# Attention and two expert layers on one core: inputs turned at a pair's end, the leaky sum kept in PSUM, a respread start and end of the second layer

## The chip, the cores and the metric

The kernel runs on one core of a Trainium2 chip. The metric is the device time of one execution in microseconds. Five engines work side by side, each through its own queue of instructions: TensorE (PE, matmuls and transposes), VectorE (DVE), ScalarE (ACT), GpSimd (POOL) and SyncE (SP, here the one that issues DMAs). Semaphores hold an instruction until what it reads is written and what it overwrites is read.

## The reference, cut to what matters

```python
scores = q @ k.T / 8 - slope * dist       # 2 batches, 8 heads, 768 tokens, 64 columns
a = softmax(where(keep, scores, -1e9))    # 8 global keys and 96 local ones
x = (a @ v)                               # as 1536 tokens x 512

h = x @ w_in                              # first layer: 512 -> 2048
x = (max(h, 0) + alpha * min(h, 0)) @ w_out           # leaky, 2048 -> 512

h = x @ w_in2                             # second layer
P = a0 + a1*h + a2*h**2 + a3*h**3
Q = 1 + abs(b0)*abs(h) + abs(b1)*h**2
out = (P / (Q + 1e-6)) @ w_out2
```

q, k, v and the output are 32-bit floats. The four weight matrices come as 64-bit floats, which the kernel reads and converts itself.

## The kernel before

**Products.** Every factor is split into a high and a low half of reduced width (names end in `hi` and `lo`): the high half is a copy to the narrow type, the low half the difference. A product is then three passes: hi x hi, lo x hi, hi x lo. So each value that enters a product costs one copy (mostly on ScalarE) and one subtraction (mostly on VectorE).

**Attention.** A slot `u` handles two steps `z` of two heads each: `scores` (L432), the mask and the row maxima on VectorE (`biased`, L447), `exponentials` on ScalarE (L454), the row sums on GpSimd (L471) and their reciprocal on VectorE (L472, a 128x4 instruction, one per slot), the scaling by GpSimd (L466). A slot later P is transposed on TensorE (L483, L485), copied from PSUM to `pt` (`copy_p`, L492 and L494), and multiplied with v (`values`, L507 and L509); `store_x` writes the result as `xhi` (ScalarE, L519) and `xlo` (VectorE, L520). New key and query blocks are transposed (`transpose_in`, L400), and `split_in` makes their high half on ScalarE (`khi` L407, `qhi` L410) and their low half on VectorE (L408, L411).

**Opening.** The first ten slots of the attention (`alone`, u = 0 to 9) run without products of the expert layers. From u = 10 on, `joint_slot(s)` (s = 0 to 15, u = 10 + s) weaves one slot of the attention (`opening`, `turning`) with one step of the first layer. Attention ends inside s = 15; then `plain_slot(s)` runs.

**Expert layers.** There are 96 steps: 48 of the leaky layer, 48 of the rational one; a step is a group of 512 tokens and 128 hidden columns. `first(n)` makes the hidden block in one PSUM bank with twelve matmuls (L735); for n below LATE = 16 this is always bank 3, later n % 3. `leaky(n)` forms the activation with two VectorE instructions (L741, L742) in the SBUF tile `act`, ScalarE copies it to `ghi` (L743), and GpSimd subtracts to `glo` (L744). `rational_a` to `rational_e` do the same for the second layer over more instructions (L753 to L786). `second(n)` multiplies with the output weights (L801), twelve matmuls into four banks. At the end of a group `drain` adds the halves of a sum (L826) and makes the next layer's inputs: `xhi` (L834) at once, `xlo` (L835) through the queue `later`.

**Weights.** `tick` is called twice per slot and moves a pipeline of weight loads: ScalarE scales the exponent word (L324, tile `de`), three VectorE instructions join the two words (L313, L314, L315, tile `dx`, called a conversion below), a tick later the high half is copied (L301 on ScalarE, L303 on GpSimd in `alone`), and another tick later VectorE makes the low half (L304). Each tick also runs one entry of `later`. Which ticks start a load stands in the table of `plan_weights`: for the second layer's first weights it names ticks 48 to 95 in part, and then every fifth from 101 on.

**Order.** Nothing is scheduled: the instructions stand on each engine in the order in which the code calls them.

Of the kernel before, what the change touches and what calls it, by code (L numbers as in the profile page):

```python
# [37 lines left out]
JOIN = 20  # L38
# [22 lines left out]
class Kernel:  # L61
# [35 lines left out]
    def arm(self, attention, sfx):  # L97
        tc = self.tc
        self.sfx = sfx
        self.slots = list(self.early)  # L100
        self.pipe, self.join, self.unspilled, self.later, self.splits = (deque() for _ in range(5))
        self.loads = self.started = self.used = 0
        moe = self.moe()
        with tc.tile_pool(name="spill_" + sfx, bufs=1, space=DRAM) as spill:
            self.spilled = [self.alloc_slot(spill, i, "d") for i in range(KEPT)]
            self.saved = {mg: spill.tile([P, NC, DM], F32, name=f"saved{mg[0]}{mg[1]}_{sfx}") for mg in SAVED}
            with tc.tile_pool(name="at_" + sfx, bufs=1) as pool:
                attention(pool, moe)
            with tc.tile_pool(name="late_" + sfx, bufs=1, reuse_waits="tile") as late:
                self.slots += [self.alloc_slot(late, i) for i in range(NEARLY, NF)]  # L110
                moe(None)
# [109 lines left out]
    def plan_weights(self):  # L221
# [26 lines left out]
        times += range(101, 160, 5)  # L248
# [35 lines left out]
    def tick(self, on_act, start, spread=False):  # L284
        nc = self.nc
        if self.later:
            self.later.popleft()()
# [74 lines left out]
    def attention_window(self, pool, moe):  # L362
# [124 lines left out]
        def copy_p(u, first_bank):  # L487
            for z in steps_of(u):
                copy = nc.vector.tensor_copy if z < JOIN - 3 and z % 4 == 0 else nc.scalar.copy
                t = transposed(z, first_bank + z % 2)  # L490
                if width(z) == P:
                    copy(pt[z % 4][:, :, 0], t[:, :, 0])  # L492
                else:
                    copy(pt[z % 4], t)  # L494
# [66 lines left out]

        def alone(u):
# [3 lines left out]
            biased(u)  # L566
            if u < 2:
# [6 lines left out]
            lows = [store_x(u - 3)]  # L574
            for n, (nm, i, cs) in enumerate(inputs(u)):
# [3 lines left out]
                if u < 2:  # L579
                    lows.pop()()  # L580
            keys_of_all(u)
            self.tick(False, t in self.starts, spread=True)
            exponentials(2 * u + 1)
            transpose_p(u - 2, 6)
            for low in lows:
                low()
            self.join_step(3)
            copy_p(u - 2, 6)
# [8 lines left out]
        def opening(u):  # L597
# [3 lines left out]
            biased(u)  # L601
            due = {JOIN // 2: (u - 3,), JOIN // 2 + 1: (u - 3, u - 2)}.get(u, (u - 2,))
# [6 lines left out]
            lows = [store_x(v) for v in due]  # L609
            for z in some[1:]:  # L610
                exponentials(z)
            for low in lows:
                low()

        def turning(u):
# [3 lines left out]
            lows = []  # L619
# [5 lines left out]
            for nm, i, cs in inputs(u):  # L625
                lows.append(split_in(nm, i, 2, cs))
            return lows
# [93 lines left out]
    def moe(self):  # L721
# [16 lines left out]
        def leaky(n):  # L738
# [3 lines left out]
            nc.vector.scalar_tensor_tensor(t, h, 0.0, t, ALU.max, ALU.add)  # L742
            nc.scalar.copy(hi, t)  # L743
            nc.gpsimd.tensor_tensor(lo, t, hi.bitcast(F32), ALU.subtract)  # L744
# [65 lines left out]
        def drain(n, d):  # L810
# [9 lines left out]
            if n == N - 1 and d == 3:  # L820
                for half in (slice(0, DM // 2), slice(DM // 2, DM)):
                    nc.vector.tensor_add(o[:, half], y[:, half], o[:, half])
                    nc.sync.dma_start(out=out[:, half], in_=o[:, half])
# [21 lines left out]
        def joint_slot(s, halves):  # L845
# [6 lines left out]
            opening(u)  # L852
            first(s)
            self.tick(True, 2 * s in self.starts)
            lows = turning(u)
            leaky(s)
            for low in lows:
                low()
            if s:
                second(s - 1)  # L860
            self.tick(True, 2 * s + 1 in self.starts)

        def plain_slot(s):
# [4 lines left out]
            if s < N:  # L868
                first(s)
            if s >= N:  # L870
                final_slot(s)
                return
# [13 lines left out]
            if ready and not steps[early][0]:  # L886
                leaky(early)
            self.tick(True, 2 * s in self.starts)
            if ready and steps[early][0]:
# [85 lines left out]
```

## Time and profile before

| | us |
|---|---|
| median of three runs (661.48, 663.15, 663.91) | 663.15 |
| the profiled execution's own time | 662.42 |
| its span in the profile | 660.62 |
| PE busy | 622.9 (94%) |
| DVE busy | 541.1 (82%) |
| ACT busy | 374.8 (57%) |
| POOL busy | 191.6 (29%) |
| mean granted TensorE clock | 0.987 of full |

Busy shares are means over stages that differ. The page cuts the span into 40 slices of 16.5 us; there TensorE is busy less than nine tenths in slices 1 to 4, 7 and 25 and in the last, and VectorE nine tenths or more in slices 6 to 8 (83 to 132 us), 14, 17, 22 to 26, 28 to 31 and 38. So the reading goes by stages: prelude to 20 us, slots of the attention alone to 59 us, joint slots to about 202 us, leaky slots to about 380 us, the rational layer, the end.

### The profile page before, as it was taken

What the parts mean: (1) busy time and instruction counts of PE and PEld (TensorE: products, weight loads), DVE (VectorE), ACT (ScalarE), POOL (GpSimd) and SP (SyncE); (2) the same over time, 40 slices, a digit from 0 to 9 for tenths busy, and PEclk for the clock granted to TensorE, in tenths of its full rate; (3) what the DMA queues carried; (4) which work ended last, traced back from release to release, by engine and by line L of the source; (5) the groups of instructions that cost most, each with busy time, mean ns of one, the idle gap of its engine ahead of it and who ended that gap; (6) DMA issues with size and microseconds to landing.
All of it is one profiled execution on the core that took longest, in us unless ns stands there. A gap on an engine that the chain in (4) does not pass through costs nothing. (4 is left out here: it accounts for less than half of the span.)

```text
span 660.6 us, 9551 instructions
## 1 busy us (share of the span) xinstructions
PE 622.9 (94%) x3250; PEld 506.3 (77%) x3250; DVE 541.1 (82%) x972; ACT 374.8 (57%) x782; POOL 191.6 (29%) x268
## 2 busy tenths in 40 slices
PE   6777998999999999999999998999999999999994
PEld 6566766778878888888888877878878888888783
DVE  4687899987656987977889999999989877786984
ACT  2785565667643432333333376777777666766662
POOL 4454434333341321222222212222222222222221
PEclk7998999999999999999999999999999999999998
DMA  8879498978777952330522511131110000300302
GB/s 162 192 189 274 145 256 261 269 207 268 255 263 253 353 183 90 103 96 32 165 90 65 158 34 33 36 125 32 33 64 1 1 1 1 127 1 0 129 0 70
DMA packets 84859, 82.82 MB, mean 125 GB/s; under 512 B 45312, under 2 KB 61952, under 8 KB 84800
## 3 DMA queue, kind: packets, MB, share of 16 engines
q1 hardware_dynamic: 84800, 82.11, 41.6%
q8 instruction: 27, 0.44, 0.3%
q14 instruction: 32, 0.26, 0.1%
HBM read 60.21 MB, written 19.92 MB: 121 GB/s over the span
## 5 line engine op out<-in xcount | busy, mean ns | idle before, releaser
L744 POOL TENSOR_TENSOR glo<-act,ghi 128x512 fp32r<-128x512 f32 x48 | 65.6, 1366 | 213.5 <-ACT ghi L743 193.8
L786 POOL TENSOR_TENSOR glo<-act,ghi 128x512 fp32r<-128x512 f32 (+1 forms) x49 | 65.3, 1332 | 201.9 <-ACT ghi L782 180.3
L743 ACT CAST ghi<-act 128x512 fp32r<-128x512 f32 x48 | 29.8, 621 | 104.6 <-DVE act L742 96.7
L735 PE MATMUL bank<-xhi,winhi_f 128*128 128x512 f32 x256 | 68.4, 389 | 0.0
L735 PE MATMUL bank<-xhi,winlo_f 128*128 128x512 f32 x256 | 68.4, 389 | 0.0
L735 PE MATMUL bank<-xlo,winhi_f 128*128 128x512 f32 x256 | 68.4, 389 | 0.0
L454 ACT ACTIVATE prob<-prob,stat 128x232 f32<-128x232 f32 (+1 forms) x96 | 44.7, 468 | 40.2 <-DVE stat L447 40.0
L735 PEld LDWEIGHTS bank<-xhi,winhi_f 128*128 128x128 f32 x256 | 48.1, 188 | 10.0
L735 PEld LDWEIGHTS bank<-xlo,winhi_f 128*128 128x128 f32 x256 | 48.1, 188 | 10.0
L735 PEld LDWEIGHTS bank<-xhi,winlo_f 128*128 128x128 f32 x256 | 48.1, 188 | 10.0
L314 DVE SCALAR_TENSOR_TENSOR dx<-de,dx 128x512 int32<-128x512 int32 x64 | 52.7, 824 | 2.2
L315 DVE SCALAR_TENSOR_TENSOR dx<-stage,dx 128x512 int32<-128x512 int32 x64 | 52.1, 815 | 2.2
L762 DVE SCALAR_TENSOR_TENSOR stage<-stage,abs_b 128x512 f32<-128x512 f32 (+1 forms) x49 | 36.2, 739 | 16.3 <-ACT stage L754 16.3
L753 ACT ACTIVATE stage<-bank 128x512 f32<-128x512 f32 (+1 forms) x49 | 28.8, 587 | 35.7 <-PE bank L735 35.7
L466 POOL TENSOR_SCALAR prob<-prob,rec 128x232 f32<-128x232 f32 (+1 forms) x96 | 42.2, 458 | 16.9 <-DVE rec L472 10.2
L782 ACT CAST ghi<-act 128x512 fp32r<-128x512 f32 (+1 forms) x49 | 30.2, 616 | 27.7 <-DVE act L779 27.7
L324 ACT ACTIVATE de<-stage 128x512 f32<-128x512 f32 x64 | 42.6, 671 | 2.6 <-DMA stage<-in_moe_w_out_dram 2.6
L801 PE MATMUL bank<-wouthi_f,glo 128*128 128x512 f32 x144 | 41.3, 392 | 0.8 <-POOL glo L786 0.7
L801 PE MATMUL bank<-wouthi_f,ghi 128*128 128x512 f32 x144 | 41.3, 392 | 0.6 <-ACT ghi L782 0.6
L313 DVE TENSOR_SCALAR dx<-de 128x512 int32<-128x512 int32 x64 | 38.6, 603 | 3.5 <-ACT de L324 3.5
L801 PE MATMUL bank<-woutlo_f,ghi 128*128 128x512 f32 x144 | 41.0, 389 | 0.0
L777 DVE SCALAR_TENSOR_TENSOR stage<-stage,cq,bank 128x512 f32<-128x512 f32 (+1 forms) x49 | 36.0, 734 | 4.1 <-ACT bank L767 4.1
(208 smaller groups left out, 1466.7 us busy)
## 6 DMA issues: line engine op xcount, KB each, us to landing
stage<-in_moe_w_in_dram SPq DMA_DIRECT2D x32, 512.0 KB, 3.9
stage<-in_moe_w_out_dram SPq DMA_DIRECT2D x32, 512.0 KB, 4.1
part<-saved_f SPq DMA_DIRECT2D x16, 256.0 KB, 4.0
va<-in_v_dram SPq DMA_DIRECT2D x13, 256.0 KB, 5.1
saved_f<-part SPq DMA_DIRECT2D x12, 256.0 KB, 3.5
out_dram<-part SPq DMA_DIRECT2D x11, 256.0 KB, 2.0
rawk<-in_k_dram SPq DMA_DIRECT2D x10, 256.0 KB, 4.6
rawq<-in_q_dram SPq DMA_DIRECT2D x10, 256.0 KB, 4.7
```

The source lines that it names most:

```text
L313: lambda: nc.vector.tensor_scalar(y, e, 3, None, ALU.logical_shift_left),
L314: lambda: nc.vector.scalar_tensor_tensor(y, e, -(2**31), y, ALU.bitwise_and, ALU.bitwise_or),
L315: lambda: nc.vector.scalar_tensor_tensor(y, low, 29, y, ALU.logical_shift_right, ALU.bitwise_or),
L324: nc.scalar.mul(self.de[n % 2], self.staged(n)[:, :, :, 1].bitcast(F32), 2.0**-112)
L454: nc.scalar.activation(p[:, j - e, :w], p[:, j - e, :w], AF.Exp, bias=st[:, j : j + 1], scale=-1.0, accum_out=st[:, 4 + j : 5 + j],)
L466: nc.gpsimd.tensor_scalar(p[:, j, :w], p[:, j, :w], r[:, e + j : e + j + 1], 1.0, ALU.mult, ALU.mult)
L735: nc.tensor.matmul(bk, w["in", a][:, c, :], x[:, c, :], start=e == 0, stop=e == len(seq) - 1)
L744: nc.gpsimd.tensor_tensor(lo, t, hi.bitcast(F32), ALU.subtract)
L762: nc.vector.scalar_tensor_tensor(w, w, self.ab[:, 0:1], ab, ALU.add, ALU.mult)
L777: nc.vector.scalar_tensor_tensor(w, w, self.cq[:, 0:1], r, ALU.add, ALU.mult)
L786: nc.gpsimd.tensor_tensor(lo, u, hi.bitcast(F32), ALU.subtract)
L801: nc.tensor.matmul(y[d], lhs, rhs, start=begin and e == 0, stop=last and e == 2)
```

## The change

Five things are changed.

1. In `alone`, the transposes of new inputs, their high halves and the copies of P stand behind both pairs of exponentials; the low halves of the inputs wait in `lows` until the next slot's row maxima (`opening` of the first joint slot calls them too). A weight's low half then comes directly behind `store_x`'s low half. All copies of P are on ScalarE.
2. In `joint_slot`, both ticks stand between the attention's opening and its turning, one ahead of `first`, one behind.
3. `leaky` writes the sum back to the PSUM bank instead of `act`; ScalarE copies from there, and the subtraction for `glo` is on VectorE, from PSUM, called after the other low halves.
4. `tick` runs an entry of `later` only in every second call; the second layer's late weight starts move from 101, 106, ... to 107, 112, ...
5. At the end, the last step's first product is issued together with the one before it, a slot earlier, and the last half of the output is sent from ScalarE's DMA queue instead of SyncE's.

```diff
-        times += range(101, 160, 5)
+        times += range(107, 160, 5)
...
     def tick(self, on_act, start, spread=False):
-        if self.later:
+        self.ticks += 1
+        if self.later and self.ticks % 2:
             self.later.popleft()()
...
         def copy_p(u, first_bank):
-                copy = nc.vector.tensor_copy if z < JOIN - 3 and z % 4 == 0 else nc.scalar.copy
+                copy = nc.scalar.copy
...
         def alone(u):
             scores(u)
             both_ready(u - 1)
             biased(u)
+            low_halves()
...
             exponentials(2 * u)
-            lows = [store_x(u - 3)]
+            low = store_x(u - 3)
+            self.tick(False, t in self.starts, spread=True)
+            exponentials(2 * u + 1)
+            low()
+            self.join_step(3)
+            transpose_p(u - 2, 6)
+            copy_p(u - 2, 6)
             for n, (nm, i, cs) in enumerate(inputs(u)):
                 bank = (3, 2)[n % 2]
                 transpose_in(nm, i, bank, cs)
                 lows.append(split_in(nm, i, bank, cs))
                 if u < 2:
-                    lows.pop()()
+                    low_halves()
             keys_of_all(u)
-            self.tick(False, t in self.starts, spread=True)
-            exponentials(2 * u + 1)
-            transpose_p(u - 2, 6)
-            for low in lows:
-                low()
-            self.join_step(3)
-            copy_p(u - 2, 6)
             self.tick(False, t + 1 in self.starts, spread=u < JOIN // 2 - 1)
...
         def leaky(n):
             nc.vector.tensor_scalar(t, h, 0.0, self.al[:, fc : fc + 1], ALU.min, ALU.mult)
-            nc.vector.scalar_tensor_tensor(t, h, 0.0, t, ALU.max, ALU.add)
-            nc.scalar.copy(hi, t)
-            nc.gpsimd.tensor_tensor(lo, t, hi.bitcast(F32), ALU.subtract)
+            nc.vector.scalar_tensor_tensor(h, h, 0.0, t, ALU.max, ALU.add)
+            nc.scalar.copy(hi, h)
+            return lambda: nc.vector.tensor_sub(lo, h, hi.bitcast(F32))
...
-                    nc.sync.dma_start(out=out[:, half], in_=o[:, half])
+                    (nc.scalar if half.start else nc.sync).dma_start(out=out[:, half], in_=o[:, half])
...
         def joint_slot(s, halves):
             opening(u)
+            if s:
+                self.tick(True, 2 * s - 1 in self.starts)
             first(s)
             self.tick(True, 2 * s in self.starts)
             lows = turning(u)
-            leaky(s)
-            for low in lows:
-                low()
+            low = leaky(s)
+            for more in lows:
+                more()
+            low()
             if s:
                 second(s - 1)
-            self.tick(True, 2 * s + 1 in self.starts)
+            if s == LATE - 1:
+                self.tick(True, 2 * s + 1 in self.starts)

         def plain_slot(s):
-            if s < N:
+            if s < N - 1:
                 first(s)
+            if s == N - 2:
+                first(s + 1)
...
-            if ready and not steps[early][0]:
-                leaky(early)
+            low = leaky(early) if ready and not steps[early][0] else None
             self.tick(True, 2 * s in self.starts)
+            if low:
+                low()
```

In the rows below, `bank_82` to `bank_89` are the PSUM banks 0 to 7, and line numbers of after are one higher than those of before up to L521, and eight to nine higher in the expert layers.

**ScalarE, one late slot of `alone` with a query block.** Before, from the slot's first exponentials on:

```order
L454 ACTIVATE prob_254,stat_260<-prob_254,stat_260 128x232 x2
L519 CAST xhi_105<-bank_84 128x2x128
L410 ACTIVATE qhi_250<-bank_85 128x512
L324 ACTIVATE de_95<-stage_91 128x512
L454 ACTIVATE prob_255,stat_260<-prob_255,stat_260 128x232 x2
L494 COPY pt_266<-bank_89 128x512
```

After, from the same instruction on:

```order
L455 ACTIVATE prob_254,stat_260<-prob_254,stat_260 128x232 x2
L520 CAST xhi_105<-bank_84 128x2x128
L325 ACTIVATE de_95<-stage_91 128x512
L455 ACTIVATE prob_255,stat_260<-prob_255,stat_260 128x232 x2
L495 COPY pt_265<-bank_88 128x512
L495 COPY pt_266<-bank_89 128x512
L411 ACTIVATE qhi_250<-bank_85 128x512
```

The query's copy moves from between the two pairs of exponentials to behind the copies of P, of which both are here now.

**VectorE, a joint slot with two conversions,** the last twelve instructions up to the reciprocal of the next slot. Before:

```order
L304 TENSOR_TENSOR winlo__112<-dx_97,winhi__111 128x512
L313 TENSOR_SCALAR dx_96<-de_95 128x512
L314 SCALAR_TENSOR_TENSOR dx_96<-de_95,dx_96 128x512
L315 SCALAR_TENSOR_TENSOR dx_96<-stage_91,dx_96 128x512
L741 TENSOR_SCALAR act_100<-bank_85,al 128x512
L742 SCALAR_TENSOR_TENSOR act_100<-bank_85,act_100 128x512
L408 TENSOR_TENSOR klo<-bank_84,khi 128x4x128
L304 TENSOR_TENSOR woutlo__126<-dx_98,wouthi__125 128x512
L313 TENSOR_SCALAR dx_97<-de_94 128x512
L314 SCALAR_TENSOR_TENSOR dx_97<-de_94,dx_97 128x512
L315 SCALAR_TENSOR_TENSOR dx_97<-stage_92,dx_97 128x512
L472 RECIPROCAL rec_264<-rec_264 128x4
```

After:

```order
L314 TENSOR_SCALAR dx_98<-de_94 128x512
L315 SCALAR_TENSOR_TENSOR dx_98<-de_94,dx_98 128x512
L316 SCALAR_TENSOR_TENSOR dx_98<-stage_90,dx_98 128x512
L305 TENSOR_TENSOR winlo__112<-dx_97,winhi__111 128x512
L314 TENSOR_SCALAR dx_96<-de_95 128x512
L315 SCALAR_TENSOR_TENSOR dx_96<-de_95,dx_96 128x512
L316 SCALAR_TENSOR_TENSOR dx_96<-stage_91,dx_96 128x512
L749 TENSOR_SCALAR act_100<-bank_85,al 128x512
L750 SCALAR_TENSOR_TENSOR bank_85<-bank_85,act_100 128x512
L409 TENSOR_TENSOR klo<-bank_84,khi 128x4x128
L752 TENSOR_TENSOR glo_104<-bank_85,ghi_102 128x512
L473 RECIPROCAL rec_264<-rec_264 128x4
```

The second conversion moves from behind the leaky activation to ahead of it, the sum goes to bank 3 instead of `act`, and the subtraction L752 takes the place in front of the reciprocal.

**VectorE, start of the second layer,** from the last addition of halves (L826, after: L834) on; `stage` and `act` are tiles of the rational activation. Before:

```order
L826 TENSOR_TENSOR part_78<-bank_89,part_78 128x512
L835 TENSOR_TENSOR xlo_109<-part_75,xhi_106 128x512
L777 SCALAR_TENSOR_TENSOR stage_92<-stage_92,cq,bank_85 128x512
L778 SCALAR_TENSOR_TENSOR stage_92<-stage_92,bank_85 128x512
L779 SCALAR_TENSOR_TENSOR act_99<-act_99,na,stage_92 128x512
L762 SCALAR_TENSOR_TENSOR stage_93<-stage_93,abs_b 128x512
L835 TENSOR_TENSOR xlo_109<-part_76,xhi_106 128x512
```

After:

```order
L834 TENSOR_TENSOR part_78<-bank_89,part_78 128x512
L785 SCALAR_TENSOR_TENSOR stage_92<-stage_92,cq,bank_85 128x512
L786 SCALAR_TENSOR_TENSOR stage_92<-stage_92,bank_85 128x512
L787 SCALAR_TENSOR_TENSOR act_99<-act_99,na,stage_92 128x512
L770 SCALAR_TENSOR_TENSOR stage_93<-stage_93,abs_b 128x512
L843 TENSOR_TENSOR xlo_109<-part_75,xhi_106 128x512
```

The low half of the first block of activations (`xlo` from `part_75`) moves behind the first piece of the rational activation.

## Rows read from the trace of the kernel before

**Rows 1.** Windows: stretch, length, engines' busy us (operations), TensorE's clock, DMA share, GB/s.
```profile
38.00:60.00 22.00, 15.03 (x159) 12.69 (x160) 20.90 (x62) 15.89 (x51) 11.73 (x26) 0.92 0.85 228
55.90:59.20 3.30, 3.30 (x20) 2.81 (x16) 3.17 (x12) 2.72 (x10) 2.19 (x4) 0.50 0.96 347
78.00:148.00 70.00, 64.67 (x432) 49.03 (x430) 62.62 (x144) 42.20 (x117) 26.80 (x52) 1.00 0.84 246
148.00:200.00 52.00, 51.93 (x369) 41.72 (x366) 31.74 (x88) 30.87 (x83) 21.12 (x37) 1.00 0.80 264
```

**Rows 2.** Timeline, TensorE: start, duration, engine, line, operation, count, [idle before<-releaser].
```profile
147.41 0.38 PE L432 MATMUL bank<-khi,qhi 64*128 64x232 f32 x2
...
149.31 1.20 PE L735 MATMUL bank<-xhi,winhi__115 128*128 128x512 f32 x4
...
156.31 0.38 PE L432 MATMUL bank<-khi,qhi 64*128 64x232 f32 x2
```

**Rows 3.** Timeline, second layer's start: TensorE's two waits, then VectorE.
```profile
391.99 0.73 PE L801 MATMUL bank<-wouthi__113,ghi 128*128 128x512 f32 x2 [1.50 <-ACT ghi L782]
...
405.11 0.72 PE L801 MATMUL bank<-wouthi__121,ghi 128*128 128x512 f32 x2 [1.87 <-ACT ghi L782]
...
388.44 0.68 DVE L835 TENSOR_TENSOR xlo<-part,xhi 128x512 fp32r<-128x512 f32 x1
...
397.88 1.52 DVE L313 TENSOR_SCALAR dx<-de 128x512 int32<-128x512 int32 x1
```

**Rows 4.** Timeline, the end: TensorE, then SyncE's queue.
```profile
634.47 0.84 PE L735 MATMUL bank<-xhi,winhi_f 128*128 128x512 f32 x3
...
652.17 0.39 PE L801 MATMUL bank<-wouthi_f,glo 128*128 128x512 f32 x1
...
653.07 1.44 SPq L823 DMA_DIRECT2D out_dram<-part  x2
```

**Rows 5.** Timeline, opening slot: VectorE's mark, ScalarE's copy and its next.
```profile
37.77 0.18 DVE L472 RECIPROCAL rec<-rec 128x4 f32<-128x4 f32 x1 [1.17 <-POOL rec L471]
...
35.29 0.58 ACT L407 CAST khi<-bank 128x512 fp32r<-128x512 f32 x1
35.77 0.67 ACT L324 ACTIVATE de<-stage 128x512 f32<-128x512 f32 x1
```

**Rows 6.** Timeline, a later opening slot: VectorE, then GpSimd.
```profile
41.22 0.42 DVE L520 TENSOR_TENSOR xlo<-bank,xhi 128x256 fp32r<-128x256 f32 x1
...
42.15 0.68 DVE L494 COPY pt<-bank 128x512 f32<-128x512 f32 x1
...
41.39 0.62 POOL L303 TENSOR_SCALAR winhi__111<-dx 128x512 fp32r<-128x512 f32 x1 [1.35 <-DVE dx L315]
```

**Rows 7.** Timeline, TensorE's longest wait in the opening.
```profile
55.24 0.44 PE L507 MATMUL bank<-pt,va 128*64 128x128 f32 x4 [4.03 <-DVE pt L494]
```

**Rows 8.** Timeline, VectorE, the first joint slot.
```profile
68.39 1.51 DVE L313 TENSOR_SCALAR dx<-de 128x512 int32<-128x512 int32 x1
...
71.27 0.17 DVE L472 RECIPROCAL rec<-rec 128x4 f32<-128x4 f32 x1
```

**Rows 9.** Timeline, VectorE, a joint slot with two conversions.
```profile
118.45 0.68 DVE L408 TENSOR_TENSOR klo<-bank,khi 128x512 fp32r<-128x512 f32 x1
119.04 0.68 DVE L304 TENSOR_TENSOR woutlo__118<-dx,wouthi__117 128x512 fp32r<-128x512 f32 x1
119.64 1.52 DVE L313 TENSOR_SCALAR dx<-de 128x512 int32<-128x512 int32 x1
...
122.91 0.39 DVE L447 CUSTOM_DVE_ANT_0 prob<-bank,bm 128x232 f32<-128x232 f32 x1
...
125.37 0.42 DVE L313 TENSOR_SCALAR dx<-de 128x512 int32<-128x512 int32 x1
...
128.55 0.68 DVE L411 SCALAR_TENSOR_TENSOR qlo<-bank,qhi 128x512 fp32r<-128x512 f32 x1
```

**Rows 10.** Timeline, GpSimd in that slot.
```profile
119.32 1.55 POOL L744 TENSOR_TENSOR glo<-act,ghi 128x512 fp32r<-128x512 f32 x1 [4.87 <-ACT ghi L743]
```

More of the change, by code (lines that the diff above doesn't have):

```diff
@@ L101, in arm @@
         self.pipe, self.join, self.unspilled, self.later, self.splits = (deque() for _ in range(5))
-        self.loads = self.started = self.used = 0
+        self.loads = self.started = self.used = self.ticks = 0
         moe = self.moe()
@@ L560, in attention_window, with low_halves @@
         load_va(1)
+        lows = []
+        def low_halves():
+            while lows:
+                lows.pop(0)()
         def alone(u):
@@ L601, in opening @@
             biased(u)
+            low_halves()
             due = {JOIN // 2: (u - 3,), JOIN // 2 + 1: (u - 3, u - 2)}.get(u, (u - 2,))
@@ L608, in opening @@
                 exponentials(z)
-            lows = [store_x(v) for v in due]
+            outs = [store_x(v) for v in due]
             for z in some[1:]:
                 exponentials(z)
-            for low in lows:
+            for low in outs:
                 low()
@@ L618, in turning @@
             transpose_p(u - 1, 0)
-            lows = []
+            some = []
             for nm, i, cs in inputs(u):
@@ L625, in turning @@
             for nm, i, cs in inputs(u):
-                lows.append(split_in(nm, i, 2, cs))
-            return lows
+                some.append(split_in(nm, i, 2, cs))
+            return some
         for u in range(JOIN // 2):
@@ L855, in joint_slot @@
             lows = turning(u)
-            leaky(s)
-            for low in lows:
-                low()
+            low = leaky(s)
+            for more in lows:
+                more()
+            low()
             if s:
                 second(s - 1)
-            self.tick(True, 2 * s + 1 in self.starts)
+            if s == LATE - 1:
+                self.tick(True, 2 * s + 1 in self.starts)
         def plain_slot(s):
```

## The prediction

> **What bounds the kernel now.** I read the busy shares by stretch first, then the waits of TensorE, then one slot of each stage on every engine. A late stretch of the attention opening and the joint stage show the pattern: VectorE is busy 62.62 of 70 us between 78 and 148 us, TensorE 64.67, and TensorE's granted clock is 1.00 there but 0.92 in 38 to 60 us [rows 1]. In that stretch VectorE sets the pace, and after about 148 us TensorE does, at 8.90 us a slot [rows 2]. In the rest of the kernel TensorE is nearly always busy, apart from two waits at the start of the second layer [rows 3] and the end [rows 4]. So work on VectorE costs time from about 38 to 148 us and again near 390 to 405 us; elsewhere it is hidden behind TensorE.
>
> **Opening, up to the mark at 37.77 us.** I use the reciprocal L472 as the mark of a slot: it waits for GpSimd's sum, which waits for ScalarE's last exponential [rows 5]. The key or query copy (L407, 0.58 us, the next instruction 0.48 us after it starts) stands between the two pairs of exponentials, so it lengthens this loop. The change puts it behind the second pair. Four slots end at the 37.77 mark: 4 x 0.48 = 1.9 us. The bounds are 0 (ScalarE's own sum per slot, now with all P copies, becomes the limit) and 2.3 (4 x 0.58). I take **-1.8**.
>
> **Opening, 37.77 to 59.69 us.** VectorE loses its P copies here, two of 0.68 us, about 0.6 of it before the next one starts [rows 6]. But in two slots the weight's low half (L304) now comes straight after the 0.34 us subtraction L520, while GpSimd's high half (L303) starts 0.17 us after the conversion and takes 0.62 us [rows 6]: some 0.5 us of new waiting in each, and as much for the reciprocal in a third. That eats the two copies. Against it stands one slot without a key copy in its loop. I take **-0.3**, between -1.5 and +1.5. TensorE's 4.03 us wait for VectorE's P copy [rows 7] goes, since ScalarE has that copy ready early; what is late next is the input transpose, whose bank is read by a low half that now follows the next row maxima, about 3 us after TensorE runs dry. [...]
>
> **First joint slot, 59.69 to 71.27 us.** The reciprocal at 71.27 stands behind a whole conversion, 2.88 us from 68.39 on [rows 8]. The tick moves behind the next slot's opening, so this goes from the chain; VectorE's copy of P goes too (0.6), and the new subtraction for glo comes in (0.6): **-2.8** (bounds -2.0 and -3.2). Up to this mark: -1.8 - 0.3 + 0.7 - 2.8 = -4.2.
>
> **Joint slots with two conversions.** One slot of VectorE is 10.10 us, 118.45 to 128.55 [rows 9]. In it the first L313 takes 1.52 us, and the same instruction later 0.42, because GpSimd's L744 runs from 119.32 for 1.55 us [rows 10]: L313 ends when L744 ends. The change takes L744 off GpSimd (-1.10) and gives VectorE a subtraction of a PSUM and an SBUF operand; L408 has that form, 0.68 us, the next start 0.59 after it (+0.6). It waits for ScalarE's copy, which starts when the sum is written; the key or query low half stands between and covers all but 0.1. New slot: 10.10 - 1.10 + 0.60 + 0.10 = 9.70. The sum written back into PSUM has no row; by the nearest ones it costs from 0.1 less to 0.4 more than L408, the nearest form [rows 9], and I take 0.
>
> [...]
>
> There is a new wait as well: the first product of the next slot writes the same bank (before LATE there is only one), so TensorE must now wait until the subtraction has read it. Queued behind that product are the transposes of P and the second product. With VectorE at 9.70 us against TensorE's 8.90 this wait becomes the form in which VectorE bounds TensorE; in slots with one conversion VectorE needs a conversion less, 1.8 us (2.88 [rows 8] less the 1.10), so at most 7.9, and nothing waits. Seven slots have two conversions: the first without two L304 and with one more L520 and some wait for it (9.7 - 1.2 + 0.5 = 9.0), two on 128 columns instead of 232 (L447 takes 0.39 us on 232 [rows 9]; I estimate 0.1 less for each of four: 9.3), four at 9.7; then 7.0 us of TensorE from the first product to the next scores, 149.31 to 156.31 [rows 2]. Together 9.0 + 18.6 + 38.8 + 7.0 = 73.4, against 147.41 - 71.27 = 76.1 before: **-2.7**. At 0.4 more per slot it is +0.1, at 0.3 less, where TensorE is the bound in part, -4.6.
>
> **Leaky slots without attention.** TensorE has no idle there; ScalarE's and VectorE's forms change under its cover: 0.
>
> **Start of the second layer.** Two waits of TensorE, 1.50 and 1.87 us [rows 3]. VectorE runs without a break before both. The first low half of the activations (L835, 0.6) moves behind the first result, so the first wait falls to 0.9. Before the second, the conversion at 397.88 (its first step 1.52, all of it 2.9, as in [rows 8]) moves six half-slots on, and one more L835 moves out: 3.5 us less on VectorE, more than 1.87. Sum **-2.5** (bounds -1.5 and -3.3, the later conversions now falling on other slots).
>
> **End.** The last first product now runs one second product earlier. ScalarE can take its magnitudes before the previous result is due, instead of holding the copy L782 up. From 634.47 six groups of twelve matmuls, 0.225 us apart (three take 0.84, one 0.39), would end at 650.8 (6 x 2.70 and 0.16 of the last one's run), while the last matmul ends at 652.56 [rows 4]: 1.7 us of waiting, of which I give back 0.5 for the last low half: **-1.2**. SP's last two issues take 1.44 us together; the second goes to ScalarE's queue, idle by then. No row shows an issue from there. Bounds +0.3 and -0.9; I take **-0.4**. [...]
>
> **Sum.** -4.2 - 2.7 - 2.5 - 1.2 - 0.4 = -11.0 us. The profiled execution took 662.42 us (span 660.62 and 1.80 around it), the median is 663.15. So 651.4 for that execution and about **652.0** as a median. A difference under 0.5%, 3.3 us, is about what a measurement of this kernel cannot tell from none.
>
> **Rivals.**
> - *The joint stage gives nothing* (chance 0.25). VectorE's new wait for ScalarE's copy, held behind the P copies, takes back what GpSimd's stall cost, and slot 0 gains only half. For it: the slot is one long VectorE chain, and ScalarE now has both ticks' work ahead of the copies. Against: ScalarE is busy only 42.20 of 70 us there [rows 1]. Time: 663.2 - 2.8 (1.4 of the opening, 1.4 of slot 0) - 2.5 (layer) - 1.6 (end) = 656.3.
> - *The edits don't meet the bound* (0.09). The opening is limited by something the marks don't show (its loads, or ScalarE's sum), the low half costs what it saves, and only the later layer and the end gain, in part: 663.2 - 2.5 = 660.7, within 0.5%.
> - *The held bank binds everywhere* (0.04), the slower side. If the sum in PSUM and its two readers cost x us more a slot than I took, the seven slots lose x each, and eight slots with one conversion lose x - 1.0 once x exceeds 1.0, since TensorE's next first product waits for the low half. At x = 2.0: 14.0 + 8.0 = 22, so 652 + 22 = 674. It is slower than before from about x = 1.3 on (9.1 + 2.4 = 11.5). Against it: all forms seen are within 0.1 us of each other.
>
> **How the numbers follow.** The forecast, with terms near their values, has 0.62. Its own range is 648 to 655.5 (terms at their ends do not all fall together). The 0.25 of the first rival reaches to 658.5; beyond that 0.13, below 648 some 0.06. Range **648.0 to 658.5**. Faster by over 0.5% (below 659.8): 0.62 + 0.25 = 0.87; the same 0.09; slower 0.04.
>
> **What would show it.** After: L313 at 0.42 us throughout the joint stage; VectorE's slot near 9.7 us and scores of the slot now at 147.41 about 7 us earlier; no TensorE wait of 4 us for P; one wait near 0.9 us instead of 1.50 and 1.87; the last matmul some 1.2 us closer to the start of the last six groups. I am wrong if TensorE waits for glo in slots with one conversion, if VectorE waits over 0.3 us for ScalarE's copy in each slot, or if the clock falls more than once between 30 and 65 us.

## The result

| | median us | runs | ratio to before, 95% interval |
|---|---|---|---|
| before | 663.53 | 661.48 to 664.06 | |
| changed | 652.38 | 652.20 to 652.99 | 0.9839 [0.9817, 0.9862] |

The change takes 11.15 us off the median; 11.0 had been forecast. The two profiled executions are 10.0 us apart (spans 660.62 and 650.6). The total agrees much better than its terms do, as the table near the end shows.

### The profile page after: what moved, and what is told of

Read it like the earlier page. It is cut to its first block, busy times and chain, and to the rows that moved or that the text cites. A ratio compares the mean times of both kernels' runs of the same rounds, so it can differ in the third digit from the quotient of the medians.

```text
span 650.6 us, 9534 instructions
## 1 busy us (share of the span) xinstructions
PE 619.0 (95%) x3250; PEld 507.8 (78%) x3250; DVE 535.2 (82%) x1015; ACT 377.4 (58%) x787; POOL 126.1 (19%) x220
## 5 line engine op out<-in xcount | busy, mean ns | idle before, releaser
L751 ACT CAST ghi<-bank 128x512 fp32r<-128x512 f32 x48 | 28.2, 588 | 110.6 <-DVE bank L750 93.0
L315 DVE SCALAR_TENSOR_TENSOR dx<-de,dx 128x512 int32<-128x512 int32 x64 | 48.2, 754 | 2.2
L752 DVE TENSOR_TENSOR glo<-bank,ghi 128x512 fp32r<-128x512 f32 x48 | 33.1, 689 | 16.8 <-ACT ghi L751 9.4
L316 DVE SCALAR_TENSOR_TENSOR dx<-stage,dx 128x512 int32<-128x512 int32 x64 | 44.3, 692 | 2.2
L749 DVE TENSOR_SCALAR act<-bank,al 128x512 f32<-128x512 f32 x48 | 35.8, 745 | 12.1 <-PE bank L743 12.1
L770 DVE SCALAR_TENSOR_TENSOR stage<-stage,abs_b 128x512 f32<-128x512 f32 (+1 forms) x49 | 36.0, 737 | 11.6 <-ACT stage L762 11.5
```

Source lines behind the costliest of these rows:

```text
L315: lambda: nc.vector.scalar_tensor_tensor(y, e, -(2**31), y, ALU.bitwise_and, ALU.bitwise_or),
L316: lambda: nc.vector.scalar_tensor_tensor(y, low, 29, y, ALU.logical_shift_right, ALU.bitwise_or),
L749: nc.vector.tensor_scalar(t, h, 0.0, self.al[:, fc : fc + 1], ALU.min, ALU.mult)
L752: return lambda: nc.vector.tensor_sub(lo, h, hi.bitcast(F32))
L770: nc.vector.scalar_tensor_tensor(w, w, self.ab[:, 0:1], ab, ALU.add, ALU.mult)
```

## The profile after

The page's line of busy times of the changed kernel:

```profile
PE 619.0 (95%) x3250; PEld 507.8 (78%) x3250; DVE 535.2 (82%) x1015; ACT 377.4 (58%) x787; POOL 126.1 (19%) x220
```

GpSimd lost a third of its work (191.6 to 126.1), the other engines little. Windows of the changed kernel, with the columns of [rows 1]:

```profile
56.90:60.20 3.30, 3.30 (x30) 2.93 (x28) 2.11 (x12) 2.70 (x9) 1.95 (x5) 0.50 1.13 352
76.00:143.00 67.00, 61.47 (x427) 49.45 (x425) 61.35 (x153) 43.11 (x117) 13.52 (x35) 1.00 0.90 267
380.43:623.01 242.58, 240.66 (x1057) 197.83 (x1056) 218.26 (x314) 174.78 (x293) 60.35 (x44) 1.00 0.12 40
```

The stretch from 76 to 143 us answers to 78 to 148 us before: VectorE is still busy 92% of it. The half clock (granted 0.50) comes at nearly the same time as before, now under the scores and the product of P and v of the first joint slot. The last row reaches from the output product of the last leaky step to one 28 us before the end: 242.58 us, against 246.86 between the same two before:

```profile
384.89:631.75 246.86, 241.68 (x1058) 197.57 (x1056) 219.69 (x316) 175.20 (x295) 59.90 (x44) 1.00 0.12 39
```

VectorE in a joint slot with two conversions, as [rows 9]:

```profile
106.36 0.17 DVE L473 RECIPROCAL rec<-rec 128x4 f32<-128x4 f32 x1
...
109.20 0.42 DVE L314 TENSOR_SCALAR dx<-de 128x512 int32<-128x512 int32 x1
...
111.59 0.42 DVE L314 TENSOR_SCALAR dx<-de 128x512 int32<-128x512 int32 x1
...
115.51 0.69 DVE L752 TENSOR_TENSOR glo<-bank,ghi 128x512 fp32r<-128x512 f32 x1
116.12 0.17 DVE L473 RECIPROCAL rec<-rec 128x4 f32<-128x4 f32 x1
```

Mark to mark it is 9.76 us, where 10.10 stood and 9.70 was forecast. Both conversions begin with a short L314 now. The grouped view of that line, 76 to 143 us (count, then shortest, median and longest in ns):

```profile
L314 DVE TENSOR_SCALAR dx<-de x13: 418/420/443, 80.2 to 139.6; 128x512 int32<-128x512 int32 x13
```

Before, the same group had 12 of them, from 420 to 1520 ns. TensorE has a new wait in these slots, though not the one that was named:

```profile
95.99 0.66 PE L508 MATMUL bank<-pt,va 128*64 128x128 f32 x8 [0.98 <-DVE klo L409]
```

The product of P and v waits 0.98 us (0.8 to 1.5 in five such slots) for the low half of the key or the query, which VectorE now reaches only behind both conversions and which reads the bank that this product writes. At the start of the second layer one wait is left of the two in [rows 3]:

```profile
386.99 1.20 PE L809 MATMUL bank<-wouthi__113,ghi 128*128 128x512 f32 x4 [0.97 <-ACT ghi L790]
```

The end, as [rows 4], on TensorE, SyncE's queue and ScalarE's queue:

```profile
642.17 0.40 PE L809 MATMUL bank<-wouthi_f,glo 128*128 128x512 f32 x1
```

```profile
643.07 1.14 SPq L831 DMA_DIRECT2D out_dram<-part  x1
```

```profile
643.40 0.37 ACTq L831 DMA_DIRECT2D out_dram<-part  x1
```

## The experiments

Every kernel was timed together with the kernel before on the same chip. "Changed" is 652.38 us. An interval of a ratio is about 0.002 wide to either side, 1.3 us, so differences of a microsecond or two between kernels rest on the traces.

### Part 1 undone: the opening

```diff
-                copy = nc.scalar.copy
+                copy = nc.vector.tensor_copy if z < JOIN - 3 and z % 4 == 0 else nc.scalar.copy
...
             exponentials(2 * u)
-            low = store_x(u - 3)
-            self.tick(False, t in self.starts, spread=True)
-            exponentials(2 * u + 1)
-            low()
-            self.join_step(3)
-            transpose_p(u - 2, 6)
-            copy_p(u - 2, 6)
+            lows = [store_x(u - 3)]
             for n, (nm, i, cs) in enumerate(inputs(u)):
...
             keys_of_all(u)
+            self.tick(False, t in self.starts, spread=True)
+            exponentials(2 * u + 1)
+            transpose_p(u - 2, 6)
+            for low in lows:
+                low()
+            self.join_step(3)
+            copy_p(u - 2, 6)
```

> The changed kernel with its first part undone: in the opening the inputs are turned between the two pairs of exponentials, their low halves stay in their own slot, VectorE makes its old share of the copies of P; all else as changed (652.4 us). In the trace of the changed kernel the reciprocal at 59.69 us came 2.2 us earlier, but the scores of the second joint slot only 1.0 us. Theory: TensorE's chain through the first joint slot, part of it at half clock, sets that slot, so undoing costs only about 1 us: 653.4, range 652.9 to 654.0. Rival, the prediction's own steps: the opening is worth its whole 1.8 + 0.3 and slot 0 follows VectorE's mark: 654.5 or more.

Measured: 651.73 us (651.30 to 652.76), ratio 0.9815 [0.9799, 0.9832]. Undoing it cost nothing, less than either expectation. Three of these four runs had mean granted clocks of 0.991 to 0.994, above all runs of the changed kernel (0.980 to 0.988); the fourth, at 0.984, took 652.76 us. So the medians alone do not part the order from the clock. The scores, then the first product of the first joint slot on TensorE, changed kernel:

```profile
56.37 0.67 PE L401 MATMUL bank<-part,rawk 128*128 128x128 f32 x4 [3.35 <-DVE qlo L412]
56.97 0.56 PE L433 MATMUL bank<-khi,qhi 64*128 64x232 f32 x2
...
60.66 0.74 PE L743 MATMUL bank<-xhi,winhi__111 128*128 128x512 f32 x2 [0.20 <-DVE klo L409]
```

And with the old opening:

```profile
59.16 0.56 PE L433 MATMUL bank<-khi,qhi 64*128 64x232 f32 x2
...
61.35 0.73 PE L736 MATMUL bank<-xhi,winhi__111 128*128 128x512 f32 x2
```

In the changed kernel the scores start 2.19 us earlier, but the first product only 0.69: from the one to the other it is 3.69 us against 2.19, because all of the scores and nearly all of the product of P and v now run at half clock, and the first product waits another 0.20 us. With the old opening the transposes of P and the first half of the scores stand at that place. The marks L473 tell the same, changed kernel first:

```profile
57.49 0.18 DVE L473 RECIPROCAL rec<-rec 128x4 f32<-128x4 f32 x1 [0.23 <-POOL rec L472]
...
68.04 0.17 DVE L473 RECIPROCAL rec<-rec 128x4 f32<-128x4 f32 x1
```

```profile
59.76 0.18 DVE L473 RECIPROCAL rec<-rec 128x4 f32<-128x4 f32 x1 [0.55 <-POOL rec L472]
...
69.13 0.17 DVE L473 RECIPROCAL rec<-rec 128x4 f32<-128x4 f32 x1
```

The slot takes 10.55 us against 9.37. So 2.3 us won at the first mark are 1.1 at the next one. And 10.55 is a short one. The half clock at this place lasts about 3.3 us here and in all three profiled executions with the old opening, but 7 to 10 us in six of the eleven with the new one. In two of these six the instructions up to here are the changed kernel's (parts 4 and 5 undone, below), and their slot takes 12.83 and 11.82 us.

### Part 2 undone: the ticks of a joint slot

```diff
             opening(u)
-            if s:
-                self.tick(True, 2 * s - 1 in self.starts)
             first(s)
...
                 second(s - 1)
-            if s == LATE - 1:
-                self.tick(True, 2 * s + 1 in self.starts)
+            self.tick(True, 2 * s + 1 in self.starts)
```

> The changed kernel with its second part undone: in a joint slot one tick stands behind the first product and one behind the second, as before the change. Theory: VectorE's slot has the same instructions in another order, so slots with two conversions stay within 0.2 us of 9.76; TensorE's wait for the low half of a key or query (0.8 to 1.5 us before the values product) goes and a wait before the transposes of P comes back; the first joint slot gets a conversion into its VectorE chain but is set by TensorE: +0 to +1, 652.4 to 653.4. Rival, the prediction's step for slot 0: the conversion returns to the chain, +2.8: 655.2.

Measured: 651.98 us (651.35 to 653.18), ratio 0.9824 [0.9805, 0.9843]: no difference. The slots are again 9.76 us, and the short conversions stay:

```profile
L314 DVE TENSOR_SCALAR dx<-de x13: 419/420/443, 78.3 to 139.2; 128x512 int32<-128x512 int32 x13
```

The first slot's mark and the two marks of the eighth slot:

```profile
70.17 0.17 DVE L473 RECIPROCAL rec<-rec 128x4 f32<-128x4 f32 x1
...
128.35 0.17 DVE L473 RECIPROCAL rec<-rec 128x4 f32<-128x4 f32 x1
...
136.32 0.17 DVE L473 RECIPROCAL rec<-rec 128x4 f32<-128x4 f32 x1
```

The first slot has the conversion in its chain again, and its mark comes at 70.17 us instead of 68.04. The eighth slot has one conversion less and takes 7.97 us instead of 9.76. The scores after it start at 143.13 us, against 143.04 in the changed kernel. So part 2 moves a conversion from one slot to another within the stage that VectorE sets, and takes none out of it.

### Part 3 undone: the sum in PSUM and glo on VectorE

```diff
-            nc.vector.scalar_tensor_tensor(h, h, 0.0, t, ALU.max, ALU.add)
-            nc.scalar.copy(hi, h)
-            return lambda: nc.vector.tensor_sub(lo, h, hi.bitcast(F32))
+            nc.vector.scalar_tensor_tensor(t, h, 0.0, t, ALU.max, ALU.add)
+            nc.scalar.copy(hi, t)
+            nc.gpsimd.tensor_tensor(lo, t, hi.bitcast(F32), ALU.subtract)
+            return lambda: None
```

> The changed kernel with its third part undone: the leaky sum goes to SBUF and GpSimd subtracts glo. Theory: GpSimd's subtraction stretches a VectorE instruction beside it by about 1.1 us a slot and VectorE saves its own 0.61 and a wait of 0.14, so slots with two conversions go from 9.76 to about 10.1: seven times 0.34 is 2.4, 654.8, range 654 to 656. Rival: with the ticks where they are now GpSimd's subtraction lies beside the reciprocal and the row maxima and stretches nothing, and VectorE is 0.75 shorter: 652.4 - 5 = 647.5.

Measured: 667.74 us (667.04 to 669.41), ratio 1.0055 [1.0039, 1.0072]: slower than before, and neither expectation. GpSimd at the end of a slot:

```profile
113.20 1.26 POOL L752 TENSOR_TENSOR glo<-act,ghi 128x512 fp32r<-128x512 f32 x1 [7.60 <-ACT ghi L751]
114.55 0.19 POOL L472 TENSOR_SCALAR rec<-stat 128x4 f32<-128x4 f32 x1
```

VectorE's marks around it:

```profile
103.91 0.18 DVE L473 RECIPROCAL rec<-rec 128x4 f32<-128x4 f32 x1 [1.79 <-POOL rec L472]
...
114.78 0.18 DVE L473 RECIPROCAL rec<-rec 128x4 f32<-128x4 f32 x1 [1.77 <-POOL rec L472]
```

GpSimd takes its subtraction (here L752) when ScalarE's copy is there, at the slot's end; the row sums L472 stand behind it in its queue, and the reciprocal waits for them, 1.77 us. The slot is 10.87 us instead of 9.76, and a slot with one conversion, which waits as long, 9.63 instead of 8.56. Before the change the second conversion stood between the leaky sum and the reciprocal and covered this. The window shows what else comes of it:

```profile
76.00:143.00 67.00, 59.38 (x372) 46.16 (x372) 50.59 (x129) 39.59 (x106) 20.17 (x46) 0.95 0.81 234
```

VectorE is busy for 50.59 us instead of 61.35, and the clock falls again within the stretch (0.95).

### Parts 2 and 3 undone together

Edit: the last two diffs in one kernel.

> The changed kernel with its second and third parts both undone: ticks of a joint slot as before, the leaky sum in SBUF, glo on GpSimd. Undoing the ticks alone cost nothing, undoing the sum alone cost 15 us, because GpSimd's subtraction then stood ahead of the row sums on its queue and the reciprocal on VectorE waited 1.8 us a slot. Theory: with the old ticks a conversion again covers that subtraction, and slots with two conversions return to 10.1 us from 9.76: 652.4 + 2.2 = 654.6, range 654 to 656. Rival: the wait of the reciprocal stays even so, 660 or more.

Measured: 656.78 us (656.14 to 658.63), ratio 0.9907 [0.9881, 0.9933], 4.4 above the changed kernel and 0.8 above the range expected. The slots are 10.10 us again, with the old conversions:

```profile
L314 DVE TENSOR_SCALAR dx<-de x12: 418/963/1520, 78.5 to 135.5; 128x512 int32<-128x512 int32 x12
```

Half of them take 3.6 times as long, as in [rows 9]. So parts 2 and 3 gave 4.4 us in the joint stage, its first slot included. Part 3 alone gives all of it (undoing part 2 costs nothing), and part 2 alone, 667.74 against 656.78, costs 11.

### The sum in SBUF, glo still on VectorE

```diff
-            nc.vector.scalar_tensor_tensor(h, h, 0.0, t, ALU.max, ALU.add)
-            nc.scalar.copy(hi, h)
-            return lambda: nc.vector.tensor_sub(lo, h, hi.bitcast(F32))
+            nc.vector.scalar_tensor_tensor(t, h, 0.0, t, ALU.max, ALU.add)
+            nc.scalar.copy(hi, t)
+            return lambda: nc.vector.tensor_sub(lo, t, hi.bitcast(F32))
```

> The changed kernel with the leaky sum in SBUF, as before the change, but glo still on VectorE (from SBUF). It takes away the hold on the PSUM bank of the first product and both readers of PSUM. Theory: moving the subtraction off GpSimd is the whole gain, and where the sum stands does not matter: within 0.7 us of 652.4. Rival (the bank held until VectorE has read it keeps TensorE waiting, or an operand in PSUM costs VectorE more): 1.5 us or more faster, below 650.9.

Measured: 652.13 us (651.54 to 652.79), ratio 0.9833 [0.9812, 0.9854]. The subtraction from SBUF, 60 to 143 us:

```profile
L752 DVE TENSOR_TENSOR glo<-act,ghi x8: 681/692/693, 67.0 to 134.8; 128x512 fp32r<-128x512 f32 x8
```

And from PSUM, changed kernel:

```profile
L752 DVE TENSOR_TENSOR glo<-bank,ghi x8: 681/691/692, 67.4 to 135.0; 128x512 fp32r<-128x512 f32 x8
```

The same to a nanosecond or two, and the held bank costs nothing. The gain is GpSimd's subtraction leaving GpSimd, not the place of the sum.

### Part 4 undone, and half of it

```diff
-        times += range(107, 160, 5)
+        times += range(101, 160, 5)
...
-        if self.later and self.ticks % 2:
+        if self.later:
```

> The changed kernel with its fourth part undone: the low halves of the activations are taken at every tick and the late weight starts stand at 101, 106 and so on. Theory from the trace: the part gave 4.3 us (TensorE's waits of 1.50, 1.87, 0.67 and 0.81 us became one of 0.97 and one of 0.67, the rest lay in smaller ones): 656.7, range 656.0 to 657.2. Rival, the prediction's step: 2.5 us, 654.9.

Measured: 657.96 us (657.33 to 658.82), ratio 0.9908 [0.9892, 0.9925], 5.6 above the changed kernel and 0.8 above the range expected. In this execution the clock fell once more in the second layer, behind the two waits, and for longer in the opening, though the instructions in the opening are those of the changed kernel:

```profile
54.20:64.40 10.20, 8.66 (x42) 6.86 (x43) 4.86 (x20) 6.50 (x22) 3.58 (x10) 0.50 0.76 229
402.40:405.70 3.30, 3.30 (x9) 2.58 (x8) 3.19 (x6) 2.70 (x5) 1.38 (x1) 0.50 0.00 0
```

The starts alone, the first pair of lines:

> The changed kernel with half of its fourth part undone: the second layer's late weight starts stand at 101, 106 and so on again, the low halves of the activations keep to every second tick. Undoing both cost 5.6 us. Theory: the conversion that stood before the second wait of TensorE (1.9 us) and one before a wait of 0.8 us come back, the first wait stays near 1 us: +2.7 to +3.5, 655.1 to 655.9. Rival: the low halves were the cause and the starts give nothing: 652.4 to 653.

Measured: 657.49 us (657.03 to 659.30), ratio 0.9916 [0.9892, 0.9941]: 5.1 of the 5.6, more than either expected. Here the clock falls where it does in the changed kernel's trace, and the two spans are 5.2 us apart, so the clock does not explain the difference. VectorE there:

```profile
392.24 1.51 DVE L314 TENSOR_SCALAR dx<-de 128x512 int32<-128x512 int32 x1
...
399.94 1.79 DVE L305 TENSOR_TENSOR winlo_f<-dx,winhi_f 128x512 fp32r<-128x512 f32 x1
```

TensorE behind it:

```profile
399.46 1.19 PE L809 MATMUL bank<-wouthi__121,ghi 128*128 128x512 f32 x4 [1.25 <-ACT ghi L790]
...
405.98 1.21 PE L809 MATMUL bank<-wouthi__125,ghi 128*128 128x512 f32 x4 [0.72 <-ACT ghi L790]
...
412.58 1.20 PE L809 MATMUL bank<-wouthi_f,ghi 128*128 128x512 f32 x4 [0.77 <-ACT ghi L790]
```

VectorE has no idle time between the pieces of the rational result; a conversion of 2.9 us or a low half of 1.79 puts each next piece off by its whole length, and TensorE waits 1.25, 0.72 and 0.77 us in turn, then 0.76 and 0.80 more near 430 and 486 us. The other edit, the activations' low halves at every second tick, is worth what the first wait shows: it stays at 0.97 here and is 1.49 with both undone.

### Part 5 undone: the end

```diff
-                    (nc.scalar if half.start else nc.sync).dma_start(out=out[:, half], in_=o[:, half])
+                    nc.sync.dma_start(out=out[:, half], in_=o[:, half])
...
-            if s < N - 1:
+            if s < N:
                 first(s)
-            if s == N - 2:
-                first(s + 1)
```

> The changed kernel with its fifth part undone: the last first product at its old place, both last output halves from SyncE's queue. Theory: TensorE's last six groups of matmuls end 1.2 us later, and the queue gives nothing (from the last matmul to the end it is 8.06 us before and 8.04 after): 653.6, range 653.2 to 654.0. Rival, the prediction's step with 0.4 for the queue: 654.0 or more, with the last packets landing 0.4 later behind the last matmul.

Measured: 654.62 us (653.73 to 655.46), ratio 0.9869 [0.9848, 0.9891]. The median lies where the rival stood. The last matmul, then SyncE's last issues:

```profile
643.93 0.40 PE L809 MATMUL bank<-wouthi_f,glo 128*128 128x512 f32 x1
```

```profile
644.82 2.08 SPq L831 DMA_DIRECT2D out_dram<-part  x2
```

From the output product at 623.50 to the end of the last matmul it is 20.83 us, 1.27 more than in the changed kernel (623.01 to 642.57). From that matmul to the end it is 8.72 us with both halves on SyncE's queue, 8.06 before the change, and 7.5 to 8.4 in the twelve profiled executions with ScalarE's queue. The longest of these tails is the one of this run, yet before, with the same two issues, it is no longer than with ScalarE's queue. So whether the queue is worth some tenths is not settled.

### TensorE's wait of 3.35 us taken away

```diff
             self.tick(False, t + 1 in self.starts, spread=u < JOIN // 2 - 1)
+            if u == JOIN // 2 - 2:
+                low_halves()
```

> The changed kernel with one edit: in the last but one slot of the opening the low half of the query is made at the end of the slot, and not behind the next row maxima. TensorE's 3.35 us wait for it (56.37 us in the trace of the changed kernel) should go. Theory: the fall of the granted clock that follows this wait goes with it, and the first joint slot, where TensorE leads, gets some 1.0 to 1.7 us shorter: 651.0, range 650.5 to 651.6. Rival: TensorE only waits elsewhere or the clock falls all the same: 652.0 to 652.8.

Measured: 654.47 us (652.68 to 655.80), ratio 0.9860 [0.9831, 0.9889]: not faster, and slower than either expectation. TensorE has other waits in its place, 1.14 us at 56.18 for the same low half and 1.57 us at 59.66 for ScalarE's copy of P.

The granted clock fell all the same, and once more where this kernel's instructions are those of the changed one:

```profile
26.80:33.60 6.80, 6.56 (x38) 5.37 (x38) 3.27 (x14) 5.54 (x20) 2.67 (x8) 0.50 1.18 279
60.90:67.70 6.80, 6.09 (x16) 4.83 (x17) 1.64 (x5) 2.38 (x10) 0.93 (x3) 0.50 0.52 116
```

The changed kernel in the first of these stretches:

```profile
26.80:33.60 6.80, 6.37 (x71) 5.17 (x72) 4.66 (x23) 6.74 (x24) 3.55 (x10) 1.00 0.94 236
```

So the clock falls there without that one wait too, and where it falls in the opening differs from execution to execution. Its cause stays open.

### The weight's low half ahead of the attention's

```diff
                 exponentials(z)
+            while self.splits:
+                self.splits.popleft()()
             for low in outs:
                 low()
```

> The changed kernel with one edit: in a joint slot the weight's low half that is waiting goes to VectorE ahead of the attention output's low half, which waits 0.48 us for ScalarE there. No instruction is added or taken away. Theory: VectorE sets the slots with two conversions, so seven slots get up to 0.48 us shorter, 3.4 us: 649.0, range 648.5 to 650. Rival: TensorE's wait for the key or query low half before the values product (0.8 to 1.5 us a slot) sets the slot, and filling VectorE's idle time gives nothing: 652.4.

Measured: 650.22 us (649.47 to 650.77), ratio 0.9802 [0.9782, 0.9822], a little short of the gain expected. VectorE in one slot:

```profile
115.34 0.17 DVE L473 RECIPROCAL rec<-rec 128x4 f32<-128x4 f32 x1
...
116.67 0.86 DVE L305 TENSOR_TENSOR woutlo__118<-dx,wouthi__117 128x512 fp32r<-128x512 f32 x1
117.46 0.41 DVE L521 TENSOR_TENSOR xlo<-bank,xhi 128x256 fp32r<-128x256 f32 x1
...
124.71 0.17 DVE L473 RECIPROCAL rec<-rec 128x4 f32<-128x4 f32 x1
```

The slot is 9.37 us, 0.39 shorter: the wait of 0.48 for the attention's high half is filled, and part of that goes back, since the weight's low half itself takes 0.86 instead of 0.68 beside GpSimd's scaling. From the second mark of the joint stage to its end the trace gains 2.75 us. So VectorE is what sets these slots. The intervals of this kernel and the changed one overlap a little, so that it beats it rests on the trace as well.

### The same with part 1 undone

Edit: the diff above and that of part 1.

> The kernel with the weight's low half ahead of the attention output's (650.2 us) with the opening put back to how it stood before the change. Theory: the opening's new order gives up to 0.9 us in TensorE's chain but as much is lost when the granted clock falls, so nothing is gained or lost: 649.5 to 650.9. Rival, the prediction's step: the opening is worth 1.4 or more: 651.6 or more.

Measured: 650.67 us (650.34 to 651.21), ratio 0.9810 [0.9793, 0.9828]. Again the opening's new order neither gains nor loses: in the two traces it is 2.3 us ahead at the first mark (57.45 against 59.74) and loses 2.4 in the first joint slot (11.79 against 9.38).

### One more VectorE instruction to ScalarE

On top of the low half's new place; `nal` is a constant, `al` times -1.

```diff
-            nc.vector.tensor_scalar(t, h, 0.0, self.al[:, fc : fc + 1], ALU.min, ALU.mult)
-            nc.vector.scalar_tensor_tensor(h, h, 0.0, t, ALU.max, ALU.add)
+            nc.scalar.activation(t, h, AF.Relu, scale=self.nal[:, fc : fc + 1])
+            nc.vector.scalar_tensor_tensor(h, h, 0.0, t, ALU.max, ALU.subtract)
```

> The changed kernel with the weight's low half ahead of the attention output's (650.2 us when run alone) and one more edit: alpha * min(h, 0) is made on ScalarE, as minus Relu of -alpha * h (the same number where alpha is not negative, as the reference draws it), so VectorE has one instruction of 0.78 us less in each leaky step. Theory: VectorE's slot with two conversions falls from 9.37 to 8.6, below the 8.9 of TensorE, which then sets the pace: 7 slots times 0.45 is 3.2, 647.0, range 646 to 648. Rival: the sum now waits for ScalarE, which has the copies of P and the key or query copy ahead of it, and VectorE stands idle for as long: 650 to 651.

Measured: 651.38 us (650.62 to 655.35), ratio 0.9838 [0.9806, 0.9870]. The rival was right about the wait; the median lies 0.4 above its range. VectorE from the mark on:

```profile
105.95 0.17 DVE L475 RECIPROCAL rec<-rec 128x4 f32<-128x4 f32 x1
...
113.56 0.70 DVE L754 SCALAR_TENSOR_TENSOR bank<-bank,act 128x512 f32<-128x512 f32 x1 [0.91 <-ACT act L753]
```

ScalarE's last two ahead of that:

```profile
112.34 0.60 ACT L410 CAST khi<-bank 128x512 fp32r<-128x512 f32 x1
112.82 0.71 ACT L753 ACTIVATE act<-bank,nal 128x512 f32<-128x512 f32 x1
```

VectorE has one instruction less and waits 0.91 us for the one that ScalarE does in its place, behind the key's copy. The slot is 9.57 us, 0.20 longer than with the low half's new place alone.

## Why the prediction was right

The mechanisms of three terms were right: GpSimd's stall of VectorE in the slots with two conversions, the loads and low halves at the second layer's start, and the end. Their sizes were not all right, and the errors cancelled: the opening and the joint stage gave 2.6 us less than forecast, the second layer 1.8 more. That the medians meet the total to 0.2 us is luck; the two profiled executions miss it by 1.0.

| term | forecast | from the traces | cost when undone (medians) |
|---|---|---|---|
| opening to 59.69, with the clock | -1.4 | -2.2 at the mark | -0.7 |
| first joint slot | -2.8 | -1.0 | with the next row: +4.4 |
| slots with two conversions | -2.7 | -1.1 | |
| second layer's start | -2.5 | -4.3 | +5.6 |
| end | -1.2 | -1.3 | with the next row: +2.2 |
| DMA queue | -0.4 | 0.0 | |

The costs when undone add up to 11.5 us, against the 11.15 of the whole change, so no large part is left unexplained, though each is known to about 1.3 us only.

- **Opening.** The marks came 1.9 us earlier at 37.77 (-1.8 forecast) and 0.3 more at 59.69 (-0.3). The wait for P's copy went, and the input transpose was late next, by 3.35 us. What failed is the +0.7 that the sum holds for the clock: no run shows this term by itself. What the runs showed in its place is that the fall came again (granted clock 0.50 from 56.9 to 60.2 us) and hit TensorE's chain into the first product, 1.5 us (3.69 against 2.19); in other executions it lasted longer still. And the mark on VectorE was taken as the gain although TensorE leads from there on. Undone, part 1 is worth nothing that can be measured.
- **First joint slot.** The conversion did leave the chain, but 10.55 us were left, not 8.8: half clock ahead of the first product, and P's four copies on ScalarE alone, behind which the query's high half waits. With the old opening the slot is 9.37, which is -2.2 against before: the term was nearly right by itself and was paid back by part 1. The conversion that left came back in the eighth slot. The prediction counts that slot among its seven, so its sum holds, but moving the ticks gained nothing.
- **Slots with two conversions.** The slot came to 9.76 (9.70 forecast): the stall of L313 went, the subtraction costs 0.61 and a wait of 0.14 for ScalarE. (In [rows 9] and [rows 10] L313 ends 0.29 us after L744 and not with it; the sum does not need that.) Mis-sized were the first of the seven (9.56 for 9.0: it waits 1.03 us for the attention's high half), the two on 128 columns (9.50 for 9.3, a wait of 0.63 instead of 0.48) and the last stretch (7.41 for 7.0), with the 0.06 of each other slot 1.6 us in all. The wait for glo's bank, by which VectorE was to bound TensorE and which was one of the rivals, did not bind; the run with the sum in SBUF is the same. The wait that took its place is for the low half of the key or the query in the bank of P and v. VectorE is busy meanwhile, and with the old ticks this wait is gone and the time the same, so it costs nothing by itself.
- **An operand in PSUM.** By one of the expectations it might cost VectorE more than one in SBUF. The subtraction L752 took 691 ns from PSUM against 692 from SBUF, and the kernel with the sum in SBUF is no faster (652.13 us against 652.38): the traces show no surcharge for this form.
- **Second layer.** The forecast was too small since only two waits were taken. The starts at 101 and every fifth tick after it put each conversion and its low half in front of a rational result; the waits of 0.67 and 0.81 us near 433 and 489 us went with them, and one of 0.67 near 470 us came. By the windows TensorE's idle time there fell from 5.18 to 1.92 us, 3.3 of the 4.3; the rest lies in what the trace counts as busy.
- **End.** Right: 1.25 us at the last matmul. The queue, put at 0.4, gave nothing that can be seen between before and after.

## What to carry to other kernels

When work moves off an engine, look at what stood behind it in that engine's queue and at what runs beside it on others: here the same subtraction stretched a VectorE instruction by 1.1 us in one order, and in another, with the row sums behind it, kept VectorE waiting 1.8 us in each slot. A mark on one engine tells a gain only as long as that engine leads; follow it to the engine that ends the stage. Taking an instruction out of one slot gains nothing if it comes back in another slot that the same engine sets. Where an engine runs without idle time into a result that another waits for, move other work out of its way there: here moving the weight loads was worth 5.1 us, and halving the rate of the small low halves about 0.5.

## What the runs showed of the hardware

- The same instructions ran at half clock (granted 0.50) at different places in different executions: 26.8 to 33.6 us in one kernel, not in the changed one (1.00), and 54.2 to 64.4 us instead of 56.9 to 60.2 in another. The changed kernel's runs had mean granted clocks from 0.980 to 0.988, those with part 1 undone 0.984 to 0.994, and those with the weight's low half moved as well 0.983 to 0.985. Why was not settled.
- Beside GpSimd's subtraction of two tensors VectorE's L314 took 1.52 us instead of 0.42, and an L305 1.79 instead of 0.68; beside GpSimd's scaling by one column an L305 took 0.86.
